# Attention and gated experts in one kernel: P summed in place, row maxima transposed on VectorE, 512-key tiles, 20 P buffers and a new order

## The chip, the cores and the metric

The kernel runs on one core of one Trainium2 chip. The metric is the device time of one execution in microseconds; a run's figure is that of its only core. "Before" is the median of three runs.

## What is computed

First an attention over 8 batches and 8 heads, with 1152 keys, head size 64, and queries averaged in pairs to 576. Its output, laid out as 8 x 576 x 512, goes into a layer of four causal attention experts, of which each token uses two, with weights from a gate.

```python
# attention
q_pool = q.reshape(B, H, S // 2, 2, D).mean(axis=3)          # 8, 8, 576, 64
scores = scale * np.matmul(q_pool, k.transpose(0, 1, 3, 2))  # ..., 576, 1152
scores = scores - np.max(scores, axis=-1, keepdims=True)
attn = np.exp(scores)
attn = attn / (np.sum(attn, axis=-1, keepdims=True) + 1e-09)
x = np.matmul(attn, v)        # then heads side by side: 8, 576, 512
# experts: 4 heads of 64, causal, top 2 of 4 by x @ w_gate
q, k, v = x @ wq[e], x @ wk[e], x @ wv[e]
a = softmax(where(causal, -1e9, scale * q @ k.T))
out += mask[..., None] * w[:, :, kk:kk + 1] * (a @ v @ wo[e])
```

## The kernel before

The kernel works on 32 *head pairs* p: two heads stand one above the other on the 128 partitions, 64 rows each. Every four head pairs make one batch b, whose expert part follows while later head pairs already run.

**Precision by splitting.** A 32-bit matrix product is made from rounded parts: K is `kh` plus the rest `kl`, Q is `qh` plus `ql`. Scores are kh·qh + kl·qh + kh·ql, and a fourth matmul (`ON` with `RM`) subtracts the row maximum. So each pair of matmuls (one for each head) appears four times for a chunk of 128 keys and a half of the queries (256 or 320, `QB`).

**One head pair, in stages.**

- `f_loadq`, `f_loadk`, `f_loadv` issue loads on SP's queue. K comes in three tiles of 384 keys. `f_prepq` adds the two queries of a pair on VectorE, ScalarE rounds the sum to `qh`, VectorE subtracts for `ql`; `f_prepk` makes `kh` on ScalarE and `kl` on GpSimd. `QD` holds the last 64 queries of both heads side by side.
- `f_max` computes rough scores kh·qh, 128 queries x 384 keys for each head, into PSUM (`gen`, eight banks), and VectorE reduces each to a column of maxima in `PM` (`row_max`, L602). `f_mxs` does the same for `QD` with one full-size matmul.
- `f_rows` takes the maximum over the three tiles (L648, `nm`), transposes it on TensorE with an identity matrix (L652), copies the rows to SBUF on VectorE (L657, `nt`), and two DMAs put them into rows 0 and 64 of `RM`.
- `f_st` makes the transposed scores of a half of the queries, one or two key chunks at a time, and ScalarE writes the exponentials into a P buffer (`pt`, L696). There are 11 P buffers (`NPT`).
- `f_av` multiplies P with V (L362, accumulated in one bank over nine chunks) and adds P to `sacc` (`add_up`): the first chunk is copied there by ScalarE (L371), the other eight are added by GpSimd (L379). A P buffer is free when both have read it.
- `g_norm`, after the ninth chunk: VectorE folds `sacc` by 32 columns and transposes (`fold32`, L739), a small matmul with `fold` sums over partitions (L764, the denominators), then a reciprocal, a transpose and a product; `f_xfin` splits the result into `x`.

**The experts** (`f_qk`, `f_vproj`, `f_mmax`, `f_mst`, `f_mask`, `f_mav`, `f_yfin`, `f_out`) take the same steps for each batch: projections in 12 matmuls each (L346), maxima with the causal mask (L1001), exponentials (L1044), a triangle cut on GpSimd (L1063), and the output product.

**What sets the order.** All these are Python generators ("flows"). A loop at the end of the kernel function picks, at each step, the flow that is ready first by an estimate of each engine's clock (`clk`, advanced by `emit` with a cost for each instruction), and writes its instructions down. A flow has a mode A, B or C by the shape of its matmuls: A for 64 rows x 128 columns (`rows2`, L355), B for 128 x 64 (`cols2` L362, and L764), C for 128 x 128 (`mm` L346, and L652). The loop prefers flows of the mode that it is in. `PLAN` has a row of 13 numbers for every half head pair (`GR` = 2) with thresholds for this choice: how long to wait for a flow of the present mode, how many P chunks must wait before a switch to P·V, when maxima and experts are due. A `Ring` is a set of buffers; a flow that needs one is not ready before the estimate says that one is free.

Of the kernel before, what the change touches and what calls it, by code (L numbers as in the profile page):

```python
# [17 lines left out]
SQ = 576  # L18
NKC = 9
# [12 lines left out]
NPT, NSA = 11, 3  # L32
# [29 lines left out]
    (0.2, 0.3, 0.6, 6, 4, 2.0, 0.12, 0.02, 3, 4.5, 3.9, 4.6, 4.55),  # L62
    (0.2, 0.3, 0.6, 6, 4, 2.0, 0.12, 0.02, 3, 4.5, 3.9, 4.6, 4.55),
    (0.15, 0.45, 0.2, 1, 2, 1.4, 0.25, 0.04, 2, 4.05, 3.9, 4.05, 4.1),
    (0.15, 0.45, 0.2, 1, 2, 1.4, 0.25, 0.04, 2, 4.05, 3.9, 4.05, 4.1),
    (0.2, 0.6, 0.6, 2, 4, 0.7, 0.25, -0.04, 1, 4.05, 3.9, 4.6, 4.1),
    (0.05, 0.3, 0.6, 4, 2, 0.9, 0.3, -0.04, 4, 4.05, 3.9, 4.6, 4.1),
    (0.05, 0.3, 0.6, 4, 2, 0.9, 0.3, -0.04, 4, 4.05, 3.9, 4.6, 4.1),
    (0.05, 0.3, 0.6, 4, 2, 0.9, 0.3, -0.04, 4, 4.05, 3.9, 4.6, 4.1),
    (0.2, 0.6, 0.6, 2, 4, 0.7, 0.25, -0.02, 1, 4.5, 3.9, 4.6, 4.1),  # L70
    (0.2, 0.6, 0.6, 2, 4, 0.7, 0.25, -0.02, 1, 4.5, 3.9, 4.6, 4.1),
    (0.05, 0.3, 0.6, 4, 2, 0.9, 0.3, -0.04, 4, 4.05, 3.9, 4.6, 4.1),
    (0.15, 0.45, 0.2, 1, 2, 1.4, 0.25, 0.04, 2, 4.05, 3.9, 4.05, 4.1),
    (0.05, 0.3, 0.6, 4, 2, 0.9, 0.3, -0.04, 4, 4.05, 3.9, 4.6, 4.1),
    (0.05, 0.3, 0.6, 4, 2, 0.9, 0.08, -0.04, 4, 4.05, 3.9, 4.6, 4.1),
    (0.1, 0.45, 0.3, 4, 2, 2.0, 0.12, 0.06, 1, 4.05, 3.9, 4.05, 4.1),
    (0.1, 0.45, 0.3, 4, 2, 2.0, 0.12, 0.06, 1, 4.05, 3.9, 4.05, 4.1),
    (0.05, 0.3, 0.6, 4, 2, 0.9, 0.3, -0.04, 4, 4.05, 3.9, 4.6, 4.1),
    (0.05, 0.3, 0.6, 6, 2, 0.9, 0.3, -0.04, 2, 4.05, 3.9, 4.6, 4.1),
    (0.05, 0.3, 0.6, 6, 2, 0.9, 0.3, -0.04, 2, 4.05, 3.9, 4.05, 4.1),  # L80
    (0.05, 0.3, 0.6, 4, 2, 0.9, 0.3, -0.04, 4, 4.05, 3.9, 4.6, 4.1),
    (0.05, 0.3, 0.6, 4, 2, 0.9, 0.3, -0.04, 4, 4.05, 3.9, 4.6, 4.1),
    (0.05, 0.3, 0.6, 4, 2, 0.9, 0.3, -0.04, 4, 4.05, 3.9, 4.6, 4.1),
    (0.05, 0.3, 0.6, 4, 2, 0.9, 0.3, -0.04, 4, 4.05, 3.9, 4.05, 4.1),
    (0.15, 0.45, 0.1, 2, 2, 1.2, 0.02, -0.3, 3, 4.05, 2.9, 4.6, 4.55),
    (0.1, 0.6, 0.45, 1, 2, 0.7, 0.3, -0.2, 3, 4.5, 2.9, 4.05, 4.75),
    (0.05, 0.3, 0.6, 6, 2, 0.9, 0.3, -0.04, 2, 4.05, 3.9, 4.05, 4.1),
    (0.05, 0.3, 0.6, 6, 2, 0.9, 0.3, -0.04, 2, 4.05, 3.9, 4.05, 4.1),
    (0.05, 0.3, 0.6, 4, 2, 0.9, 0.3, -0.04, 4, 4.05, 3.9, 4.05, 4.1),
    (0.05, 0.3, 0.6, 4, 2, 0.9, 0.3, -0.04, 4, 4.05, 3.9, 4.05, 4.1),  # L90
    (0.05, 0.3, 0.6, 4, 2, 0.9, 0.3, -0.04, 4, 4.05, 3.9, 4.05, 4.1),
    (0.1, 0.3, 0.2, 3, 2, 1.0, 0.12, -0.3, 2, 4.5, 2.9, 4.05, 4.75),
    (0.1, 0.3, 0.2, 3, 2, 1.0, 0.12, -0.3, 2, 4.5, 2.9, 4.05, 4.75),
    (0.05, 0.3, 0.6, 4, 2, 0.9, 0.3, -0.04, 4, 4.05, 3.9, 4.05, 4.1),
    (0.05, 0.1, 0.45, 3, 2, 1.2, 0.02, -0.3, 2, 4.05, 2.9, 4.6, 4.55),
    (0.05, 0.3, 0.6, 4, 2, 0.9, 0.3, -0.04, 4, 4.05, 3.9, 4.05, 4.1),
    (0.05, 0.3, 0.6, 4, 2, 0.9, 0.3, -0.04, 4, 4.05, 3.9, 4.05, 4.1),
    (0.05, 0.3, 0.6, 4, 2, 0.9, 0.3, -0.04, 4, 4.05, 3.9, 4.05, 4.1),
    (0.05, 0.3, 0.6, 4, 2, 0.9, 0.08, -0.04, 4, 4.05, 3.9, 4.6, 4.1),
    (0.05, 0.3, 0.6, 4, 2, 0.9, 0.08, -0.04, 4, 4.05, 3.9, 4.6, 4.1),  # L100
    (0.05, 0.3, 0.6, 6, 2, 0.9, 0.3, -0.04, 4, 4.05, 3.9, 4.05, 4.1),
    (0.15, 0.1, 0.2, 1, 1, 1.0, 0.02, -0.1, 4, 4.05, 3.9, 4.05, 4.55),
    (0.2, 0.6, 0.6, 1, 3, 1.2, 0.02, -0.3, 2, 4.5, 3.9, 4.6, 4.1),
    (0.05, 0.3, 0.6, 6, 1, 0.9, 0.3, -0.04, 4, 4.05, 3.9, 4.05, 4.1),
    (0.05, 0.3, 0.6, 6, 1, 0.9, 0.3, -0.04, 4, 4.05, 3.9, 4.05, 4.1),
    (0.05, 0.3, 0.6, 6, 2, 0.9, 0.3, -0.04, 4, 4.05, 3.9, 4.05, 4.1),
    (0.05, 0.3, 0.6, 6, 2, 0.9, 0.3, -0.04, 4, 4.05, 3.9, 4.05, 4.1),
    (0.05, 0.3, 0.6, 4, 2, 0.9, 0.08, -0.04, 4, 4.05, 3.9, 4.6, 4.1),
    (0.15, 0.3, 0.2, 2, 2, 2.0, 0.08, -0.2, 0, 4.5, 3.9, 4.05, 4.75),
    (0.05, 0.3, 0.6, 4, 2, 0.9, 0.08, -0.04, 4, 4.05, 3.9, 4.6, 4.1),  # L110
    (0.05, 0.3, 0.6, 4, 2, 0.9, 0.08, -0.04, 4, 4.05, 3.9, 4.6, 4.1),
    (0.2, 0.3, 0.6, 6, 4, 2.0, 0.12, 0.02, 3, 4.5, 3.9, 4.6, 4.55),
    (0.2, 0.3, 0.6, 6, 4, 2.0, 0.12, 0.02, 3, 4.5, 3.9, 4.6, 4.55),
    (0.05, 0.3, 0.6, 4, 2, 0.9, 0.08, -0.04, 4, 4.05, 3.9, 4.6, 4.1),
    (0.05, 0.3, 0.6, 6, 2, 0.9, 0.3, -0.04, 2, 4.05, 3.9, 4.05, 4.1),
    (0.05, 0.3, 0.6, 6, 2, 0.9, 0.3, -0.04, 2, 4.05, 3.9, 4.05, 4.1),
    (0.1, 0.45, 0.6, 6, 3, 1.0, 0.08, -0.1, 2, 4.05, 3.9, 4.6, 4.55),
    (0.05, 0.45, 0.6, 6, 2, 0.9, 0.3, -0.04, 2, 4.5, 3.9, 4.05, 4.1),
    (0.1, 0.45, 0.6, 2, 1, 1.0, 0.25, 0.06, 1, 4.05, 2.9, 4.6, 4.1),
    (0.05, 0.3, 0.6, 6, 2, 0.9, 0.3, -0.04, 2, 4.05, 3.9, 4.05, 4.1),  # L120
    (0.05, 0.1, 0.6, 1, 2, 1.0, 0.3, -0.2, 2, 4.5, 3.9, 4.6, 4.55),
    (0.05, 0.1, 0.6, 1, 2, 1.0, 0.3, -0.2, 0, 4.5, 3.9, 4.6, 4.75),
    (0.15, 0.3, 0.6, 3, 1, 0.7, 0.45, -0.3, 3, 4.05, 2.9, 4.6, 4.55),
    (0.1, 0.3, 0.45, 3, 3, 0.7, 0.02, -0.2, 0, 4.5, 3.9, 4.6, 4.1),
    (0.1, 0.3, 0.45, 3, 3, 0.7, 0.02, -0.2, 0, 4.5, 3.9, 4.6, 4.1),
    (0.15, 0.3, 0.6, 3, 1, 0.7, 0.45, -0.3, 3, 4.05, 2.9, 4.6, 4.55),
# [5 lines left out]
class Res:  # L132
# [6 lines left out]
    def __getitem__(self, i):  # L139
        return self.ap[i]  # L140

# [13 lines left out]
class Ring:  # L155
# [7 lines left out]
    def new(self):  # L163
        t = min(self.slots)
        self.slots.remove(t)
        self.live += 1
        self.n += 1

        r = Res(self.pool.tile(self.shape, self.dt, tag=f"{self.tag}{t[3]}", name=f"{self.tag}_{self.n}", bufs=1), self)
        _, r.u, r.ue, r.slot = t  # L170
        return r
# [17 lines left out]
def pooled_attention_then_moe_kernel(ctx: ExitStack, tc: tile.TileContext, qT, kT, vP, wall, wop, out):  # L189
# [64 lines left out]
    r_sacc = ring("sacc", [128, 640], F32, NSA)  # L254
    r_part = ring("part", [128, 20], F32, 4)
    r_kraw = ring("kraw", [128, 384], F32, 3)
# [3 lines left out]
    r_kh = ring("kh", [128, 384], F32R, 8)  # L260
    r_kl = ring("kl", [128, 384], F32R, 6)
    r_v = ring("v", [128, 3, 128], F32, 6)
    r_nm = ring("nm", [128, 2 * NQC], F32, 2)
    r_nt = ring("nt", [2 * NQC, 128], F32R, 2)
    r_accs = ring("accs", [128, 320], F32, 3)
    r_r9 = ring("r9", [128, 10], F32, 2)
# [102 lines left out]
    def act_first(o, i, n, R, W):  # L369

        nc.scalar.activation(o, i, AF.Copy, bias=1e-9 / 128, scale=1.0)  # L371
        emit("ACT", n / 1200 + 0.083, R, W)
# [880 lines left out]
```

## Time and profile before

| | |
|---|---|
| median of 3 runs (lowest to highest) | 1174.4 us (1174.08 to 1174.66) |
| the profiled execution | 1174.46 us, span 1172.7 us |
| granted TensorE clock | 0.997 |
| TensorE matmul / VectorE / ScalarE / GpSimd busy | 1137.2 / 883.6 / 700.6 / 969.5 us |
| DMA | 70.30 MB, mean 60 GB/s |

The page gives one execution. "PE" is TensorE's matmuls, "PEld" its weight loads, DVE is VectorE, ACT ScalarE, POOL GpSimd, SP the engine that issues the loads. A row of a group reads: line, engine, operation, output <- inputs with shapes, count, then busy time in us and mean ns of one, then idle time of the engine just before and what ended it. A row of the waits has who waited, for whom, then us in total, how often, and the longest. A row of the timeline has start and length in us and how many equal instructions were merged. A 32-bit matmul whose operands aren't rounded (P·V, denominators, transposes) leaves two records.

### The profile page before, as it was taken

To read this page: it belongs to the slowest core of one execution; us is meant where nothing else is said; L and a number is where in the kernel's file an instruction comes from. 1 tells how busy PE (TensorE), PEld (TensorE's weight loads), DVE (VectorE), ACT (ScalarE), POOL (GpSimd) and SP (SyncE) were. 2 spreads that over 40 slices of the span, in tenths; PEclk is the share of its full clock that TensorE was granted. 3 is DMA by queue.
4 is the path that set the end of the run, shared out by engine and by line. 5 is a ranking of instruction groups with operands and counts; after the bars stand their busy time and mean duration, and the time that the engine had idled before them with its cause. 6 is when DMAs were issued, how large, how long until landed. Compare 5 with 4: busy or idle time off the path is not lost.

```text
span 1172.7 us, 29459 instructions
## 1 busy us (share of the span) xinstructions
PE 1137.2 (97%) x11233; PEld 885.1 (75%) x11233; DVE 883.6 (75%) x2120; ACT 700.6 (60%) x2036; POOL 969.5 (83%) x839
## 2 busy tenths in 40 slices
PE   7999999999999999999999999999999999999997
PEld 5666787778877787777877788777887678777685
DVE  6998777786787867878588676978667876676675
ACT  4576645766466664676547755567645675556634
POOL 4899997988789977899689985899886997979922
PEclk9999999999999999999999999999999999999999
DMA  4223220121121211213102221112211123200011
GB/s 153 82 87 98 63 62 24 47 92 62 63 62 29 95 48 62 63 55 105 42 22 63 80 81 57 29 49 80 80 43 34 56 65 98 62 22 2 2 37 46
DMA packets 40569, 70.30 MB, mean 60 GB/s; under 512 B 4886, under 2 KB 31724, under 8 KB 40428
## 3 DMA queue, kind: packets, MB, share of 16 engines
q1 hardware_dynamic: 40284, 68.29, 18.7%
q8 instruction: 88, 1.44, 0.5%
q14 instruction: 53, 0.43, 0.1%
q10 hardware_dynamic: 144, 0.13, 0.0%
HBM read 58.73 MB, written 9.44 MB: 58 GB/s over the span
## 4 chain that ended last, share of the span: by engine, by line
PE 67%; POOL 20%; DVE 8%; issue 3%; ACT 2%; DMA 1%; POOLq 0%; SPq 0%; DVEq 0%; ACTq 0%
PE gen L355 30%; PE gen L362 19%; POOL sacc L379 18%; PE gen L346 17%; DVE PM L602 3%; POOL kl L379 1%; DVE gen L1001 1%; DVE part L739 1%; ACT pt L696 1%; PE gen L764 1%; POOL pt L1063 1%; PE gen L652 0%; DMA qraw<-in_qT 0%; DVE MPM L1001 0%; DVE qraw L375 0%
## 5 line engine op out<-in xcount | busy, mean ns | idle before, releaser
L379 POOL TENSOR_TENSOR sacc<-sacc,pt 128x512 f32<-128x512 f32 (+3 forms) x583 | 821.4, 1415 | 124.0 <-ACT sacc L371 81.9
L602 DVE TENSOR_REDUCE PM<-gen 128x1 f32<-128x384 f32 x864 | 425.6, 547 | 129.6 <-PE gen L355 108.5
L696 ACT ACTIVATE pt<-gen 128x320 f32<-128x320 f32 (+1 forms) x1152 | 383.1, 434 | 146.2 <-PE gen L355 140.6
L362 PE MATMUL gen<-pt,v 128*64 128x320 f32 (+4 forms) x2752 | 358.7, 404 | 1.2 <-POOL pt L1063 0.8
L362 PEld LDWEIGHTS gen<-pt,v 128*64 128x64 f32 (+1 forms) x2752 | 186.5, 137 | 118.2 <-issue 11.0
L355 PE MATMUL gen<-qh,kh 64*128 64x320 f32 (+1 forms) x1152 | 224.8, 322 | 2.9 <-DVE PM L602 1.7
L355 PE MATMUL gen<-qh,kl 64*128 64x320 f32 (+1 forms) x1152 | 207.8, 300 | 0.0
L355 PE MATMUL gen<-ql,kh 64*128 64x320 f32 (+1 forms) x1152 | 199.7, 293 | 0.0
L355 PE MATMUL gen<-RM,ON 64*128 64x320 f32 (+1 forms) x1152 | 199.7, 293 | 0.0
L355 PE MATMUL gen<-kh,qh 64*128 64x384 f32 x768 | 163.7, 378 | 8.7 <-ACT qh L366 7.0
L355 PEld LDWEIGHTS gen<-qh,kh 64*128 64x128 f32 x1152 | 143.0, 186 | 37.6 <-issue 12.4
L355 PEld LDWEIGHTS gen<-RM,ON 64*128 64x128 f32 x1152 | 138.9, 187 | 0.0
L355 PEld LDWEIGHTS gen<-ql,kh 64*128 64x128 f32 x1152 | 138.6, 187 | 0.0
L355 PEld LDWEIGHTS gen<-qh,kl 64*128 64x128 f32 x1152 | 134.3, 186 | 0.0
L355 PEld LDWEIGHTS gen<-kh,qh 64*128 64x128 f32 x768 | 91.6, 188 | 46.9 <-issue 23.5
L379 POOL TENSOR_TENSOR kl<-kraw,kh 128x384 fp32r<-128x384 f32 x96 | 102.0, 1082 | 7.2 <-ACT pt L696 4.1
L739 DVE TRANSPOSE_TENSOR_REDUCE part<-sacc 128x16 f32<-128x512 f32 (+1 forms) x96 | 73.5, 771 | 42.1 <-POOL sacc L379 41.7
L346 PE MATMUL gen<-x,WH 128*128 128x320 f32 (+1 forms) x512 | 103.6, 297 | 0.0
L346 PEld LDWEIGHTS gen<-x,WH 128*128 128x128 f32 x512 | 82.1, 188 | 0.8 <-issue 0.4
L1001 DVE CUSTOM_DVE_ANT_0 gen<-gen,mqk 64x288 f32<-64x288 f32 (+4 forms) x160 | 74.3, 502 | 7.9 <-PE gen L355 6.7
L346 PE MATMUL gen<-x,WL 128*128 128x320 f32 (+1 forms) x256 | 75.6, 295 | 0.0
L1044 ACT ACTIVATE pt<-gen 128x320 f32<-128x320 f32 (+2 forms) x224 | 64.0, 388 | 17.5 <-PE gen L355 16.9
(117 smaller groups left out, 1495.2 us busy)
## 6 DMA issues: line engine op xcount, KB each, us to landing
kraw<-in_kT SPq DMA_DIRECT2D x96, 192.0 KB
v<-in_vP SPq DMA_DIRECT2D x96, 192.0 KB
qraw<-in_qT SPq DMA_DIRECT2D x31, 576.0 KB
out<-ob SPq DMA_DIRECT2D x28, 256.0 KB
wst<-in_wall SPq DMA_DIRECT2D x8, 193.0 KB
RM<-nt SPq DMA_DIRECT2D x62, 2.5 KB
out<-ob SPq DMA_DIRECT2D x6, 128.0 KB
out<-pt SPq DMA_DIRECT2D x3, 256.0 KB
```

The lines of the kernel that those rows point to most:

```text
L346: nc.tensor.matmul(o, lhsT, rhs, start=start, stop=stop)
L355: nc.tensor.matmul(o(j), l(HEAD[j]), r(HEAD[j]), start=i == 0, stop=i == len(terms) - 1)
L362: nc.tensor.matmul(o(HEAD[j]), l(j), r(j), start=start, stop=stop)
L379: nc.gpsimd.tensor_tensor(o, a, b, op=op)
L602: nc.vector.tensor_reduce(pm[:, i, t:t + 1], ps[:, :384], axis=AX.X, op=ALU.max)
L696: nc.scalar.activation(pts[i][:, j, :qn], st[j][:, qn * i:qn * i + qn], AF.Exp, scale=0.0625)
L739: nc.vector.tensor_reduce(out, src.rearrange("p a (b r) -> p a b r", r=32), axis=AX.X, op=ALU.add, apply_transpose=True)
L764: nc.tensor.matmul(den[HEAD[j], 400:400 + k], fold, part[:, j * k:j * k + k], start=True, stop=True)
L1001: nc.vector.tensor_tensor_reduce(p, p, mqk[:m, 384 + m - w:384 + m], 1.0, LOW, ALU.add, ALU.max, pm[:m, j, c, i:i + 1])
L1044: nc.scalar.activation(pt_[:kn, j, f:qn], st[j][:kn, o - n:o], AF.Exp, scale=0.125)
L1063: nc.gpsimd.affine_select(out=sq, in_=sq, compare_op=ALU.is_ge, fill=0.0, base=0, pattern=[[0, 2], [1, kn]], channel_multiplier=-1)
```

## The change

1. **P summed in place.** `sacc` and its copy on ScalarE are gone. The P buffer of chunk 0 becomes the accumulator, kept until the fold; GpSimd adds the other chunks to it. The small constant that the copy had added to every entry is now added to the folded column by one tiny ScalarE instruction between the fold and the denominators' matmul (L809).
2. **Some chunks folded by VectorE.** `fold_in`: when the planner's clock for GpSimd is more than `OFP` = 3.0 us past that of TensorE (or of the chunk) and VectorE's is not, VectorE folds that chunk by itself into a further slot of `part` (up to three for a half), and the slots are added up before the denominators.
3. **Maxima transposed on VectorE.** `f_rows` reduces into two groups of columns of a 32-column `nm`, VectorE transposes it in blocks of 32 x 32, and four DMAs put the blocks in place. The transpose on TensorE and the copy from PSUM are gone.
4. **q split from PSUM.** VectorE sums the two queries into a PSUM bank, by halves, with a reduce over an axis of two; `qh`, `QD` and `ql` read that bank.
5. **K in tiles of 512, 512 and 128 keys** (the first head pair keeps 384). The maxima of four query chunks over the 128-key tile share a bank and one reduce.
6. **20 P buffers** for 11, 6 + 3 and 4 + 2 of `kh`/`kl` for 8 and 6; a smaller reserve for DMA descriptors.
7. **New order.** Another `PLAN`, some cost constants changed, and new orders of maxima within a head pair.

```diff
-NPT, NSA = 11, 3
+NPT, NKH = 20, 6
+NSL, OFP, OFD = 4, 3.0, 0.0
...
-    (0.2, 0.3, 0.6, 6, 4, 2.0, 0.12, 0.02, 3, 4.5, 3.9, 4.6, 4.55),
+    (0.2, 0.6, 0.1, 6, 1, 1.0, 0.25, -0.04, 0, 4.5, 2.9, 4.6, 4.1),
...
+    KT = lambda p: ((0, 384), (384, 384), (768, 384)) if p == 0 else ((0, 512), (512, 512), (1024, 128))
...
 def f_prepq(p, q):
-        any_tt(q[:, 0, :], q[:, 0, :], q[:, 1, :], ALU.add, SQ, [q], [q])
...
-        any_tt(ql.ap, q[:, 0, :], qh.ap.bitcast(F32), ALU.subtract, SQ, [q, qh], [ql])
+        for i, (a, n) in enumerate(QB):
+            qs, c = r_gen.new(), slice(a, a + n)
+            nc.vector.tensor_reduce(qs[:, :n], q[:, :, c].rearrange("p a q -> p q a"), axis=AX.X, op=ALU.add)
...
+            dve_tt(ql[:, c], qs[:, :n], qh[:, c].bitcast(F32), ALU.subtract, n, [qs, qh], [ql])
...
 def f_max(p):
+            seq = [((c,), t) for t in range(2) for c in range(NQF)] + [(range(NQF), 2)]
...
 def f_rows(pm, srcs, k, R, flags, col):
-        nc.tensor.transpose(ps[:n, :128], nm[:, :n], ident)
-        nc.vector.tensor_copy(nt[:n, :], ps[:n, :128])
+        for j, src in enumerate(srcs):
+            nc.vector.tensor_reduce(nm[:, k * j:k * j + k], src, axis=AX.X, op=ALU.max, negate=True)
+        nc.vector.transpose(nt.bitcast(F32), nm.bitcast(F32))
...
-        for r, k, part, col in dst:
-            mv(R[part:part + 1, col:col + 128 * k].rearrange("o (c q) -> o c q", c=k), nt[r:r + k, :], [nt], [R])
+        rows = R[:, col:col + 128 * k].rearrange("(h z) (c g q) -> z g h c q", h=2, c=k, g=4)
+        for g in range(4):
+            mv(rows[0, g], nt[32 * g:32 * g + 2 * k, :], [nt], [R])
...
 def f_av(p, c, hf, pt):
-            SACC[p, hf] = r_sacc.new()
+            SACC[p, hf] = pt
...
-        add_up(sacc, pt, 0, n, n, c, pool_tt)
-        pt.free()
+        if c and not fold_in(sacc, pt, n):
+            add_up(sacc, pt, 0, n, n, pool_tt)
+        if c:
+            pt.free()
...
+    def fold_in(sacc, pt, n):
+        if clk["POOL"] < max(clk["PE"], pt.rw) + OFP or clk["DVE"] > max(clk["PE"], pt.rw) + OFD:
+            return False
...
+        fold32(part[:, part.m, :2 * k].rearrange("p (a b) -> p a b", a=2), pt[:, :, :n], 2 * n, [pt], [part])
+        part.m += 1
+        return True
...
 def g_norm(acc, sacc, n, box, gate=None):
+        nc.scalar.activation(part[:, m, :2 * k], part[:, m, :2 * k], AF.Copy, bias=1e-9 / 128, scale=1.0)
```

How the order changes is seen in the programs themselves. The first place is TensorE's queue. Before, in the expert part of a middle batch, two maximum matmuls (A), a transpose (C), eight P·V matmuls (B) and again maxima and scores (A) follow each other; `mqh`, `mkh`, `MRM` are the experts' q, k and row maxima, `gen` the PSUM banks.

```order
L355 MATMUL gen_5703<-kh_4983,qh_5019 128x384
L355 MATMUL gen_5704<-kh_4983,qh_5019 128x384
L652 MATMUL gen_5709<-ident,nm_5559 10x128
L362 MATMUL gen_5713<-pt_5645,v_5096 64x256 x2
L362 MATMUL gen_5713<-pt_5646,v_5096 64x256 x2
L362 MATMUL gen_5722<-pt_5675,v_2_4615 64x320 x2
L362 MATMUL gen_5722<-pt_5690,v_2_4615 64x320 x2
L355 MATMUL gen_5732<-kh_4983,qh_5019 128x384
L355 MATMUL gen_5733<-kh_4983,qh_5019 128x384
L355 MATMUL gen_5740<-qh_4594,kh_4436 128x256
```

Here is TensorE in the changed program, in the same batch: behind a long run of scores come the three `QD` matmuls (C) and then the denominators and a whole half of P·V (B).

```order
L375 MATMUL gen_5616<-RM_95,ON 128x256
L375 MATMUL gen_5617<-RM_95,ON 128x256
L366 MATMUL gen_5632<-kh_24_4683,QD_102 128x512
L366 MATMUL gen_5635<-kh_25_4754,QD_102 128x512
L366 MATMUL gen_5638<-kh_11_4984,QD_102 128x128
L814 MATMUL gen_5641<-part_5495,fold 64x8 x2
L382 MATMUL gen_5650<-pt_5459,v_4809 64x256 x2
L382 MATMUL gen_5650<-pt_5460,v_4809 64x256 x2
L382 MATMUL gen_5650<-pt_5497,v_4809 64x256 x2
L382 MATMUL gen_5650<-pt_5498,v_4811 64x256 x2
L382 MATMUL gen_5650<-pt_5528,v_4811 64x256 x2
L382 MATMUL gen_5650<-pt_5529,v_4811 64x256 x2
```

The transpose is out of TensorE's queue, and P·V stands together. Over the whole program the mode changes 357 times before and 172 times after; the longest A runs are 102 matmuls before, and many of 168 to 184 after.

The second place is VectorE's queue around a head pair's maxima. Before, the maxima of the next head pair (`PM_99`) and a fold stand between the reduce into `nm` and the copy `nt` of the transposed rows.

```order
L602 TENSOR_REDUCE PM_100<-gen_4819 128x1
L648 TENSOR_REDUCE nm_4824<-PM_100 128x9
L602 TENSOR_REDUCE PM_99<-gen_4852 128x1
L602 TENSOR_REDUCE PM_99<-gen_4853 128x1
L602 TENSOR_REDUCE PM_99<-gen_4871 128x1
L602 TENSOR_REDUCE PM_99<-gen_4872 128x1
L602 TENSOR_REDUCE PM_99<-gen_4890 128x1
L602 TENSOR_REDUCE PM_99<-gen_4891 128x1
L739 TENSOR_REDUCE part_4896<-sacc_4712 128x16
L657 CAST nt_4900<-gen_4898 9x128
```

After, on the same engine, the two reduces and the transpose follow the last of the maxima at once.

```order
L556 TENSOR_REDUCE gen_4651<-qraw_4299 128x320
L390 TENSOR_TENSOR mkl_4634<-gen_4635,mkh_4633 128x256
L630 TENSOR_REDUCE PM_100<-gen_4658 128x1
L390 TENSOR_TENSOR ql_4628<-gen_4651,qh_4627 128x320
L630 TENSOR_REDUCE PM_100<-gen_4662 128x1
L630 TENSOR_REDUCE PM_100<-gen_4665 128x1
L677 TENSOR_REDUCE nm_121<-PM_100 128x5 x2
L681 STREAM_TRANSPOSE nt_4670<-nm_121 128x32
```

The way from the maxima to `nt` no longer leaves VectorE. Counted over the programs, GpSimd's sums of 640 elements a partition go from 285 to 212, those of 512 from 256 to 251; folds on VectorE go from 96 to 171, maxima from 864 to 678 instructions, and SP's DMAs of maxima from 98 to 196.

## Prediction before the run

> **What bounds the kernel now.** I read the page first: busy time by engine, then the chain of waits.
>
> ```profile
> span 1172.7 us, 29459 instructions
> PE 1137.2 (97%) x11233; PEld 885.1 (75%) x11233; DVE 883.6 (75%) x2120; ACT 700.6 (60%) x2036; POOL 969.5 (83%) x839
> PE 67%; POOL 20%; DVE 8%; issue 3%; ACT 2%; DMA 1%; POOLq 0%; SPq 0%; DVEq 0%; ACTq 0%
> ```
>
> TensorE is busy for 97% of the span and carries two thirds of the chain; GpSimd comes next. The 97% counts a matmul until its modelled end, so time lost between matmuls hides inside it. Starts of matmuls show it, so the second view is the timeline of PE. The program uses the array in three shapes: 64 rows x 128 columns (L355: scores and row maxima; I call it A), 128 x 64 (L362 and L764: P times V, and the denominators; B), and 128 x 128 (L346 and L652: projections, QD, transposes; C).
>
> ```profile
> 364.85 0.47 PE L355 MATMUL gen<-kh,qh 64*128 64x384 f32 x2
> 365.25 0.87 PE L362 MATMUL gen<-pt,v 128*64 128x256 f32 x8
> 366.05 0.44 PE L355 MATMUL gen<-kh,qh 64*128 64x384 f32 x2
> 366.33 0.31 PE L355 MATMUL gen<-qh,kh 64*128 64x320 f32 x2
> ...
> 368.09 0.25 PE L355 MATMUL gen<-mqh,mkh 64*128 64x192 f32 x2
> 368.18 0.28 PE L355 MATMUL gen<-mqh,mkl 64*128 64x192 f32 x2
> 368.29 0.27 PE L355 MATMUL gen<-mql,mkh 64*128 64x192 f32 x2
> ...
> 368.52 0.35 PE L355 MATMUL gen<-kh,qh 64*128 64x384 f32 x2
> 368.71 0.22 PE L355 MATMUL gen<-mqh,mkh 64*64 64x128 f32 x2
> ...
> 369.29 0.31 PE L355 MATMUL gen<-ql,kh 64*128 64x320 f32 x2
> 369.44 0.31 PE L355 MATMUL gen<-RM,ON 64*128 64x320 f32 x2
> 369.68 0.28 PE L652 MATMUL gen<-ident,nm 128*9 128x128 f32 x1
> 369.71 0.42 PE L346 MATMUL gen<-kh,QD 128*128 128x384 f32 x1
> 370.07 0.76 PE L362 MATMUL gen<-pt,v 128*64 128x320 f32 x4
> ```
>
> Read the first column. Inside a run of one shape a 384-column pair is followed after 0.19 us (368.52 to 368.71) and a 320-column pair after 0.15 (369.29 to 369.44). Where the shape changes it takes longer: A to B 0.40 instead of 0.19 (364.85 to 365.25), B to A 0.28 instead of 0.19 (seen on the first pair behind it, 366.05 to 366.33), A to C 0.24 instead of 0.15, C to B 0.36 where the 384-column pace is 0.19. The extra is 0.21, 0.09, 0.09 and 0.17: 0.14 us a change on average. In the program's order on PE the shape changes 357 times. So about 50 us of a "busy" PE is this.
>
> The third view is the waits, for what PE itself waits on.
>
> ```profile
> DVE part L739 <- POOL sacc L379: 41.7, 38, 4.2
> PEld gen L355 <- DVE PM L602: 18.2, 63, 1.1
> PE gen L764 <- DVE part L739: 9.7, 15, 1.4
> PEld gen L764 <- DVE part L739: 6.7, 12, 1.5
> ```
>
> The denominators (L764) wait for VectorE's fold, and the fold waits for the last of GpSimd's sums. The maxima (L602) hold PSUM that the next matmul wants. Nothing else holds PE for more than single microseconds, apart from the first 7 us of loading and the end.
>
> **The change, part by part.** The profiled execution took 1174.46 us, its span 1172.7; the median of the runs shown is 1174.4, so the sum is made from 1174.5.
>
> *New order and 20 P buffers.* A run of A needs one P buffer for each key chunk, so 11 buffers end it after at most 11 chunks; with 20 a whole head pair (18 chunks) goes through. Counted in the two orders, the changes of shape fall from 357 to 172: 185 fewer at 0.14 us is 26 us. Bounds: every change at the cheapest, 0.09, gives 17; at the dearest, 0.21, gives 39. I take 26. This is on PE's own line, so nothing hides it.
>
> *Transposes of the row maxima.* The 49 L652 matmuls go. The one above lets the next start after 0.03 us; its whole record is 0.28. So between 1 and 14 us; the start is the better measure of what a queued engine loses, and the waits around it are counted as changes of shape: 3 us. In their place come one more small reduce (49, see L648 below) and a VectorE transpose, beside the old CAST's place, and four DMAs for two. Those are on the path maxima, row in RM, next head pair's scores, and stand on SP's in-order queue ahead of later K, V and Q loads.
>
> ```profile
> L648 DVE TENSOR_REDUCE nm<-PM 128x9 f32<-128x27 f32 x31 | 5.7, 183 | 1.1
> L396 SPq DMA_DIRECT2D RM<-nt x62: 652/700/896, 48.0 to 1071.5; - x62
> L779 DVE STREAM_TRANSPOSE gen<-r 128x256 f32<-128x256 f32 x48 | 22.1, 460 | 3.5
> ```
>
> Two more issues are 1.4 us a set; 98 more in all are 69 us of SP's time. After the new order's last maxima (QD) stands a run of about 40 B matmuls, 8 us at the pace of the eight records at 365.25 (0.80 us; a B matmul leaves two records). The path is three maxima (L602 below, 0.55 each), two small reduces, a transpose of at most 0.46, four issues: 1.65 + 0.36 + 0.46 + 2.8 = 5.3 us, plus a landing that these rows don't show. Hidden, with some 2 us over: 0. If that cover is gone it is a rival below. For the loads behind them on SP:
>
> ```profile
> SPq L396 <- DVE nt L657: 160.5, 13, 25.8
> ACT kh L366 <- DMA kraw<-in_kT: 19.3, 18, 3.4
> ```
>
> SP already stands 160 us behind a late `nt`, K loads with it, and ScalarE waited 19 us in all for K, PE for no load. Another 1.4 us in front of a load is lost in that: 0.
>
> *K in 512-key tiles.* For a query chunk the maxima go from three 384-column pairs to two of 512 and one of 128. At 0.15 us per 320 columns a 512 pair is 0.24. For a pair of 128 there is no row; by columns it is 0.06, but 192-column pairs already stand at 0.09 to 0.11, so up to 0.11; I take that, the nearest row. 3 x 0.19 = 0.57 becomes 0.59, or at worst 0.54 becomes 0.59: 0 to +6 us over 31 x 4 chunks, QD's 31 sets up to 2 more. I take +5. The Trainium skill (TensorE: Matmul & The Clock Gate, Back-to-back issue gap) gives a sustained 81 ns for a matmul of 128 columns and 131 for 512. By its figures old and new come out level (an estimate, interpolating 384), and the sum would be 5 us lower; but its figure for a pair of 384 would be about 0.23 where the row has 0.19, so the rows stand.
>
> *P summed in place, folds on VectorE, q.* These are off PE. Their price by group:
>
> ```profile
> L379 POOL TENSOR_TENSOR sacc<-sacc,pt 128x640 f32<-128x640 f32 x285 | 461.8, 1623 | 38.8 <-ACT sacc L371 22.7 <-DVE gate L916 1.0
> L379 POOL TENSOR_TENSOR sacc<-sacc,pt 128x512 f32<-128x512 f32 x256 | 330.4, 1291 | 76.8 <-ACT sacc L371 57.4 <-ACT pt L696 3.6 <-DVE PM L602 0.7
> L602 DVE TENSOR_REDUCE PM<-gen 128x1 f32<-128x384 f32 x864 | 425.6, 547 | 129.6 <-PE gen L355 108.5 <-PE gen L346 16.2
> L739 DVE TRANSPOSE_TENSOR_REDUCE part<-sacc 128x20 f32<-128x640 f32 x48 | 40.3, 841 | 24.4 <-POOL sacc L379 24.1
> L371 ACT ACTIVATE sacc<-pt 128x640 f32<-128x640 f32 x48 | 36.8, 767 | 0.1
> L375 DVE TENSOR_TENSOR qraw<-qraw 128x576 f32<-128x576 f32 x31 | 38.8, 1252 | 10.8 <-DMA qraw<-in_qT 10.8
> L375 DVE TENSOR_TENSOR ql<-qraw,qh 128x576 fp32r<-128x576 f32 x31 | 35.5, 1145 | 4.5 <-ACT qh L366 4.5
> L375 DVE TENSOR_TENSOR x<-gen,x 128x320 fp32r<-128x320 f32 x32 | 15.4, 481 | 4.7 <-ACT x L366 4.5
> ```
>
> GpSimd: the order holds 212 sums of 640 for 285 and 251 of 512 for 256: 73 x 1.62 + 5 x 1.29 = 125 us less of 969. ScalarE: 96 copies go (0.77 for the wide ones), 96 tiny ones come. VectorE: 75 more folds (171 for 96) at up to 0.84 = 62 us; 35 small reduces and 49 more nm ones at 0.18 = 15; 678 maxima for 864 on the same columns, so only the fixed part of 186 goes, somewhere between 0 and 0.2 us each, say 20; q goes from 1.25 + 1.15 to a sum over 1152 values, by L602's 547 for 384 about 1.64, and 0.9 for the remainder from PSUM (by L375 x): +4. Net about +60, to 945 us. None of this is PE's time. What reaches PE is the wait for the last sum: with 125 us off GpSimd I take 10 of the 16.4 us that L764 waited for `part`. Ends: all 16 gone, or 10 more, where each of the 96 den pairs waits 0.1 us for the ScalarE step that now stands between the fold and it, in order behind exponentials. And with 21 instead of 27 maximum tiles a pair the 18.2 us behind `PM` shrink by a quarter: 4 (ends 9 and 0).
>
> Sum: 1174.5 - 26 - 3 + 5 - 10 - 4 = 1136.5. **Forecast 1136 us.** With each term at its better or worse half this case spans 1118 to 1152.
>
> **The rivals.**
>
> *The long runs starve on VectorE.* In A runs two engines must keep pace with PE, and VectorE gets more to do. Three such runs of today, by window:
>
> ```profile
> 627.30:632.90 5.60, 5.60 (x88) 5.42 (x86) 3.75 (x8) 4.53 (x16) 5.37 (x5) 1.00 0.15 41
> 677.40:684.70 7.30, 7.30 (x82) 6.62 (x80) 7.18 (x18) 6.61 (x18) 6.91 (x7) 1.00 0.01 2
> 752.60:761.00 8.40, 7.73 (x88) 6.78 (x88) 8.28 (x18) 6.62 (x19) 5.97 (x10) 1.00 0.11 27
> ```
>
> The columns are PE, PEld, VectorE, ScalarE, GpSimd, with counts. With VectorE at 3.75 of 5.60 us the matmuls come every 64 ns, with it full (7.18 of 7.30, 8.28 of 8.40) every 89 and 95. Some 3 ns of that are the wider matmuls; the rest, about 25 ns, is waiting. The change has 6,464 A matmuls, as before. If 17% more of them than today run at VectorE's pace, that is 6,464 x 0.17 x 0.025 = 28 us: **1164**. For it: +60 us on VectorE, and runs that give it no pause. Against: fewer, wider maxima, and a B run of 8 us behind each long A run in which VectorE catches up. The Trainium skill (SBUF — State Buffer, Door 1: The DMA port swizzle) says that an access that crosses to a new 16-byte line pays; the new q sum steps 2304 bytes between its two terms, which would bear on this case. No row of before shows such a read. Were the sum to take twice its 1.64 us, VectorE would have 51 us more.
>
> *More goes than I count.* Changes at 0.21, no added cost of the 512 tiles, the waits for `part` and half of those for `PM` gone: 1174.5 - 39 - 3 - 16 - 9 = **1107**. For it: 0.14 rests on four places, and with GpSimd lighter the fold may never be late.
>
> *The row path comes late (slower).* Place: the first scores of each of 31 head pairs, which read RM. If VectorE is over 2 us behind when QD's maxima are queued, the B run no longer covers the path; then the two extra issues, 1.4 us, and 0.4 us of extra VectorE steps are in the open each time: 31 x 1.8 = 56, giving **1192**. It decides where the lag passes those 2 us; no wait of PE for RM shows in before, against it.
>
> That the change doesn't do what it says can be put aside: the order shows the folds, the missing transposes and the 172 changes of shape.
>
> **How the numbers follow.** Forecast 0.59, starving runs 0.18, more gained 0.15, late rows 0.08. About 0.2% is what a measurement of this kernel can tell from no change. Starving runs spread from 1150 to 1182, so a quarter of that case is not faster: faster 0.87, same 0.03, slower 0.10. The range 1104 to 1172 takes in the first three cases but for that tail.
>
> **What would show it.** Right: starts at a change of shape still 0.1 to 0.2 us apart from the pace, GpSimd near 845, VectorE near 945, ScalarE near 655, waits of L764's successor for `part` under 10 us. Wrong: VectorE at 97% or more in most long A windows with matmuls 85 ns apart (starving); PE idle ahead of the first scores of a head pair behind a DMA into RM or a late `nt` (late rows); or a PE that reaches the pace of 64 ns in the long runs, with nothing left of the waits (more gained).

## The result and the profile after

The changed kernel takes **1123.1 us** (median of 4 runs, 1122.1 to 1123.6) against 1174.5 us of the kernel before on the same chip: a ratio of 0.956, 95% interval 0.9545 to 0.9578. The gain is 51.5 us where 38 were forecast; the time lies in the range, and inside the narrower one of the forecast's own case (1118 to 1152).

The page of the changed kernel, with the span, the busy times and the chain of waits:

```profile
span 1121.9 us, 29476 instructions
PE 1096.4 (98%) x11184; PEld 879.1 (78%) x11184; DVE 919.7 (82%) x2160; ACT 654.7 (58%) x2067; POOL 826.1 (74%) x761
PE 74%; DVE 20%; issue 2%; POOL 1%; ACT 1%; DMA 1%; DVEq 0%; POOLq 0%; ACTq 0%
PE gen L375 31%; PE gen L382 22%; PE gen L366 20%; DVE PM L630 8%; DVE part L767 3%; DVE gen L1051 2%; POOL pt L394 1%; PE gen L814 1%; DVE gen L556 1%; DVE gen L829 1%; DMA kraw<-in_kT 1%; DVE gen L390 1%; DVE WL L390 1%; DVE x L390 0%; DVE MPM L1055 0%
```

GpSimd has gone from 20% of the chain to 1%, and VectorE from 8% to 20%. TensorE's "busy" share hardly moved although the span is 51 us shorter: with only 49 matmuls fewer its busy time fell by 41 us, so most of the lost time was inside the busy time, as the prediction took it. The busy times were forecast at 845 (GpSimd), 945 (VectorE) and 655 (ScalarE) and are 826, 920 and 655.

The groups behind those sums, line by line (busy time, mean ns of one, idle before):

```profile
L394 POOL TENSOR_TENSOR pt<-pt,pt 128x640 f32<-128x640 f32 x212 | 332.6, 1569 | 28.1 <-ACT pt L1094 13.7 <-DVE pt L390 0.8 <-PE gen L814 0.7
L394 POOL TENSOR_TENSOR pt<-pt,pt 128x512 f32<-128x512 f32 x251 | 323.4, 1289 | 35.7 <-PE gen L382 13.2 <-PE gen L814 5.2
L630 DVE TENSOR_REDUCE PM<-gen 128x1 f32<-128x512 f32 x558 | 345.7, 679 | 53.2 <-PE gen L375 43.4 <-PE gen L366 9.4
L767 DVE TRANSPOSE_TENSOR_REDUCE part<-pt 128x20 f32<-128x640 f32 x118 | 95.7, 826 | 10.1 <-POOL pt L394 10.1
L556 DVE TENSOR_REDUCE gen<-qraw 128x320 f32<-128x640 f32 x31 | 25.8, 833 | 0.0
L556 DVE TENSOR_REDUCE gen<-qraw 128x256 f32<-128x512 f32 x31 | 21.7, 699 | 0.7 <-ACT pt L722 0.7
```

The waits that the prediction named, in the changed kernel (in all, times, longest):

```profile
DVE part L767 <- POOL pt L394: 15.4, 11, 4.8
PEld gen L375 <- DVE PM L630: 14.7, 49, 0.9
PEld gen L814 <- ACT part L809: 7.7, 15, 1.6
PE gen L814 <- ACT part L809: 2.5, 3, 1.2
```

The fold waited 41.7 us for GpSimd before and waits 15.4 now; the rows of the denominators' waits for `part` add up to 16.4 us before and 10.2 now. (A matmul and its weight load often wait through the same time; counted once, it is 14.5 and 7.7.)

**Where the 51 us came from, by starts.** I took every distance from one matmul's start to the next one's in both traces and subtracted the pace that a matmul of its shape and width keeps in an undisturbed run (0.147 us for a pair of 320 columns, 0.110 for a pair of 128). What is left over falls from 159.5 us to 103.4: at changes of shape from 67.5 to 36.0, inside runs of A from 55.5 to 48.3, inside runs of B from 22.5 to 12.3, inside runs of C from 14.1 to 6.8. So some 31 us stand at changes of shape, 25 are shorter waits elsewhere, and about 5 were given back in undisturbed pace. The figure at a change contains any wait that happens to end there; the experiments price the change alone.

### The profile page after: what moved, and what is told of

Same layout as the page of the kernel before. It is cut to its first block, busy times and chain, and to the rows that moved or that the text cites. A ratio compares the mean times of both kernels' runs of the same rounds, so it can differ in the third digit from the quotient of the medians.

```text
span 1121.9 us, 29476 instructions
## 1 busy us (share of the span) xinstructions
PE 1096.4 (98%) x11184; PEld 879.1 (78%) x11184; DVE 919.7 (82%) x2160; ACT 654.7 (58%) x2067; POOL 826.1 (74%) x761
## 4 chain that ended last, share of the span: by engine, by line
PE 74%; DVE 20%; issue 2%; POOL 1%; ACT 1%; DMA 1%; DVEq 0%; POOLq 0%; ACTq 0%
PE gen L375 31%; PE gen L382 22%; PE gen L366 20%; DVE PM L630 8%; DVE part L767 3%; DVE gen L1051 2%; POOL pt L394 1%; PE gen L814 1%; DVE gen L556 1%; DVE gen L829 1%; DMA kraw<-in_kT 1%; DVE gen L390 1%; DVE WL L390 1%; DVE x L390 0%; DVE MPM L1055 0%
## 5 line engine op out<-in xcount | busy, mean ns | idle before, releaser
L394 POOL TENSOR_TENSOR pt<-pt,pt 128x512 f32<-128x512 f32 (+4 forms) x503 | 682.9, 1363 | 69.9 <-PE gen L382 15.7
L630 DVE TENSOR_REDUCE PM<-gen 128x1 f32<-128x512 f32 (+3 forms) x678 | 403.1, 656 | 91.4 <-PE gen L375 46.1
L382 PE MATMUL gen<-pt,v 128*64 128x320 f32 (+3 forms) x2752 | 343.6, 402 | 0.5 <-DVE MPM L1051 0.2
L375 PE MATMUL gen<-qh,kl 64*128 64x320 f32 (+1 forms) x1152 | 222.8, 302 | 0.0
L375 PE MATMUL gen<-ql,kh 64*128 64x320 f32 (+1 forms) x1152 | 213.4, 294 | 0.0
L375 PE MATMUL gen<-kh,qh 64*128 64x512 f32 (+2 forms) x768 | 147.9, 367 | 7.6 <-ACT qh L386 7.0
L375 PEld LDWEIGHTS gen<-qh,kl 64*128 64x128 f32 x1152 | 148.1, 187 | 3.1
L767 DVE TRANSPOSE_TENSOR_REDUCE part<-pt 128x20 f32<-128x640 f32 (+1 forms) x171 | 131.6, 785 | 15.4 <-POOL pt L394 15.4
L394 POOL TENSOR_TENSOR kl<-kraw,kh 128x512 fp32r<-128x512 f32 (+2 forms) x96 | 95.9, 1015 | 61.8 <-PE gen L375 22.1
L386 ACT COPY accs<-gen 128x256 f32<-128x256 f32 (+1 forms) x96 | 38.5, 401 | 66.5 <-PE gen L382 65.8
```

The source lines that it names most:

```text
L375: nc.tensor.matmul(o(j), l(HEAD[j]), r(HEAD[j]), start=i == 0, stop=i == len(terms) - 1)
L382: nc.tensor.matmul(o(HEAD[j]), l(j), r(j), start=start, stop=stop)
L386: nc.scalar.copy(o, i)
L394: nc.gpsimd.tensor_tensor(o, a, b, op=op)
L630: nc.vector.tensor_reduce(pm[:, i:i + k, t], ps[:, :n * k].rearrange("p (c n) -> p c n", c=k), axis=AX.X, op=ALU.max)
L767: nc.vector.tensor_reduce(out, src.rearrange("p a (b r) -> p a b r", r=32), axis=AX.X, op=ALU.add, apply_transpose=True)
```

## The experiments

The theory at the outset (T): about 31 of the 51.5 us come from 185 fewer changes of shape. Its rival (F): a change of shape costs nothing by itself, and a lighter GpSimd is the gain. All 12 runs, in order of time, with before and the change for comparison; each was timed against the kernel before on its chip:

| run | changes of shape | us | ratio to before (95%) | granted clock |
|---|---|---|---|---|
| before | 357 | 1174.5 | | 0.997 |
| the change | 172 | 1123.1 | 0.956 (0.9545-0.9578) | 0.997 |
| e_shapesame | 172 | 1127.6 | 0.959 (0.9580-0.9609) | 0.997 |
| e_shape64r | 360 | 1153.0 | 0.982 (0.9803-0.9836) | 1.000 |
| e_tinyA | 172 | 1162.4 | 0.990 (0.9884-0.9917) | 0.998 |
| e_after_oldplan | 245 | 1162.8 | 0.990 (0.9882-0.9912) | 0.994 |
| e_after_pt19 | 209 | 1172.6 | 0.999 (0.9979-0.9998) | 0.979 |
| e_oldplan_pt14 | 308 | 1202.1 | 1.024 (1.0227-1.0258) | 0.983 |
| e_after_nofold | 223 | 1217.3 | 1.036 (1.0345-1.0376) | 0.966 |
| e_after_pt14 | 248 | 1219.1 | 1.038 (1.0360-1.0405) | 0.972 |
| e_after_tensort | 245 | 1240.3 | 1.054 (1.0507-1.0572) | 0.966 |
| e_before_newplan | 317 | 1240.7 | 1.056 (1.0529-1.0585) | 0.974 |
| e_tinyC | 725 | 1250.8 | 1.065 (1.0636-1.0668) | 0.992 |
| e_foldpool | 172 | 1260.8 | 1.074 (1.0718-1.0754) | 0.954 |

### What a change of shape costs, among P·V

```diff
 # in g_norm, behind the two matmuls of the denominators
+        nc.tensor.matmul(den[:, 420:430], ident[:64, :], ident[:64, :10], start=True, stop=True)    # e_shape64r
+        nc.tensor.matmul(den[:64, 420:430], fold, ident[:, :10], start=True, stop=True)             # e_shapesame
```

> The changed kernel with one more tiny matmul (64 rows, 10 columns, into a part of the denominators' bank that nobody reads) behind each of the 96 accumulations of the denominators; it adds nothing to the result. The run of matmuls there is of the shape of P times V (128 rows, 64 columns), so each tiny matmul adds two changes of shape: 360 in place of 172. Nothing else moves on any engine. Theory T (about 31 of the 51.5 us come from having 185 fewer changes of shape, at 0.14 to 0.21 us each): 188 x 0.14 to 0.21 = 26 to 39 us above the control run with the tiny matmul in the neighbours' shape, so 1153 to 1168 us. Rival F (a change of shape by itself costs nothing; the gain came from shorter waits behind a lighter GpSimd): within 3 us of the control, about 1128 us.

> The control: the same 96 tiny matmuls (10 columns), but in the shape of their neighbours (128 rows, 64 columns), so that the number of changes of shape stays 172. It adds nothing to the result. Both theories: 96 matmuls of 0.03 to 0.07 us each, 3 to 7 us, so 1126 to 1130 us.

1153.0 (1148.7 to 1155.1) against 1127.6 (1125.6 to 1128.2): 25.4 us for 188 more changes, **0.135 us each**, at the low end of what T gave. F's figure, within 3 us of the control, falls: nothing but the tiny matmul differs between the two. Its shape has a price of its own beside the change, though, and the control doesn't hold that: its weight loads take 184 ns for the control's 139, and the 64-row control of the next section cost 0.136 us each where this one's cost 0.047 (4.5 us for 96). If all of 0.136 is taken off, the 29.9 us above the change leave 0.09 us a change. One place in the timeline of the run with 64-row matmuls (start, length, then what; each 32-bit matmul leaves two records):

```profile
507.58 0.24 PE L814 MATMUL gen<-part,fold 128*64 128x10 f32 x4
507.75 0.39 PE L816 MATMUL gen<-ident 64*128 64x10 f32 x2
508.07 1.52 PE L382 MATMUL gen<-pt,v 128*64 128x256 f32 x12
```

and such a place in the control:

```profile
518.22 0.29 PE L814 MATMUL gen<-part,fold 128*64 128x10 f32 x4
518.36 0.20 PE L816 MATMUL gen<-ident,fold 128*64 128x10 f32 x1
518.36 0.48 PE L382 MATMUL gen<-pt,v 128*64 128x320 f32 x1
518.41 0.20 PE L816 MATMUL gen<-ident,fold 128*64 128x10 f32 x1
518.47 0.73 PE L382 MATMUL gen<-pt,v 128*64 128x320 f32 x3
```

From the tiny matmul's first record to the first P·V that has it whole behind it: 508.07 - 507.75 = 0.32 us against 518.47 - 518.36 = 0.11; and 0.17 against 0.14 ahead of it. The two changes together are worth 0.2 to 0.3 us in the place itself.

### The same among the scores

```diff
     def rows2(o, terms, R, W, tiny=None):
...
+            if tiny is not None and i == len(terms) - 1:
+                nc.tensor.matmul(tiny[:, 400:410], ident, ident[:, :10], start=True, stop=True)                # e_tinyC
+                nc.tensor.matmul(tiny[:, 400:410], ident[:64, :], ident[:64, :10], start=True, stop=True)      # e_tinyA
```

> The changed kernel with one more tiny matmul of the projections' shape (128 rows, 128 columns, 10 columns moved) behind the scores of each of the 288 chunks of 320 queries, into a part of their bank that nobody reads; it adds nothing to the result. It splits the runs of scores: 725 changes of shape in place of 172; nothing else moves on any engine. If a change costs here what it cost among the matmuls of P times V: 553 x 0.135 = 75 us above its control (by the bounds of the forecast, 0.09 to 0.21: 50 to 116 us). Rival: in runs of scores ScalarE and VectorE set the pace, so that most of it is hidden: under 40 us.

> The control of the run with 288 tiny matmuls among the scores: the same number in the scores' own shape (64 rows), so that the changes stay 172. It adds nothing to the result. 288 matmuls of 0.03 to 0.06 us each: +9 to +17 us, 1132 to 1140 us; less where scores wait anyway.

1250.8 against 1162.4: 88.4 us for 553 changes, **0.160 us each**; up to 7.5 us of it may be the granted clock, 0.992 for 0.998 (an estimate), which leaves 0.147. The rival falls: ScalarE and VectorE don't hide a change in a run of scores. The weight loads of the tiny matmuls show where some of the time goes (first the run with 128 rows, then its control; busy time, mean ns, idle before):

```profile
L377 PEld LDWEIGHTS gen<-ident 128*128 128x128 f32 x576 | 86.9, 190 | 55.8 <-issue 55.8
L377 PEld LDWEIGHTS gen<-ident 64*128 64x128 f32 x576 | 96.5, 186 | 0.0
```

The loads take the same time, but at a change of shape they begin late: 55.8 us idle for 288 tiny matmuls is 0.19 us each, where the control has none. The control itself was missed: 39 us for its 288 matmuls, 0.136 each, where 0.03 to 0.06 were expected. A lone 64-row matmul between pairs is dear here: by the starts, the first record comes 0.139 us (median) behind the last of the scores, whose own pace is 0.073. So a tiny matmul isn't small change everywhere, and without a control the price would have read 0.23.

### Fewer P buffers, and no early folds

```diff
-NPT, NKH = 20, 6
+NPT, NKH = 14, 6                # e_after_pt14
-NSL, OFP, OFD = 4, 3.0, 0.0
+NSL, OFP, OFD = 4, 1e9, 0.0     # e_after_nofold
```

> The changed kernel with 14 P buffers in place of 20 and nothing else edited; the planner then cuts the matmuls into shorter runs: 248 changes of shape in place of 172, longest run of scores 130 matmuls in place of 184, and VectorE folds 212 chunks in place of 171, so that GpSimd is lighter still. Theory T: 76 x 0.14 to 0.21 = +11 to +16, 1134 to 1139 us. Rival F (the lighter GpSimd is the gain, whatever the number of changes): GpSimd's 32 fewer additions cannot hurt, 1120 to 1126 us.

> The changed kernel with no chunk folded early by VectorE: GpSimd makes all 587 additions, as it made 583 before the change, and VectorE folds only the 96 sums; the planner's order has 223 changes of shape in place of 172. Theory T: 51 x 0.14 to 0.21 = +7 to +11, and up to +5 for longer waits for the folded sums: 1130 to 1139 us. Rival F (the lighter GpSimd is the gain): most of the 51.5 us comes back, 1155 us or more.

Both theories fail on the first: it is slower than the kernel before by 44 us, though it has 109 changes fewer and a GpSimd that is busy 783.8 us. On the second T fails, and F's "1155 us or more" holds, but the loss is far more than the whole gain. In the run without early folds, TensorE's waits for the denominators are several times those of the changed kernel (7.7 and 2.5 us there):

```profile
DVE part L767 <- POOL pt L394: 68.5, 36, 12.7
PEld gen L814 <- ACT part L809: 37.2, 32, 6.1
PE gen L814 <- ACT part L809: 24.7, 17, 5.6
```

And the clock falls behind such waits. Three stretches of 20 us of that run (columns: PE, PEld, VectorE, ScalarE, GpSimd with counts, then the granted clock):

```profile
60.00:80.00 20.00, 18.85 (x198) 14.10 (x200) 13.25 (x25) 14.74 (x47) 19.06 (x15) 1.00 0.27 83
80.00:100.00 20.00, 13.32 (x105) 7.58 (x103) 18.40 (x29) 6.45 (x20) 19.14 (x14) 0.93 0.21 58
100.00:120.00 20.00, 13.22 (x136) 11.77 (x136) 13.23 (x26) 7.85 (x28) 12.02 (x9) 0.65 0.28 90
```

and the last two in the changed kernel:

```profile
80.00:100.00 20.00, 19.49 (x201) 13.64 (x199) 19.62 (x38) 12.95 (x41) 19.21 (x15) 1.00 0.44 131
100.00:120.00 20.00, 19.91 (x228) 15.39 (x226) 19.14 (x38) 12.72 (x42) 19.14 (x14) 1.00 0.19 60
```

GpSimd is at its limit in 80 to 100 in both (19.14 and 19.21 of 20). Where VectorE doesn't take chunks over, TensorE loses a third of its time and then its clock. If all of TensorE's time stretched with the clock, 0.966 over 1216.6 us would be 41 us, against 3 at 0.997; 51 changes at 0.135 are 7; of the 94 us above the changed kernel some 49 are left to the waits themselves. (An estimate: what the clock's fall costs was not measured by itself.) But both runs also have an order made anew, so the folds need a run in which the order stays.

### The folds given back to GpSimd, in the same order

```diff
 def fold_in(sacc, pt, n):
-        fold32(part[:, part.m, :2 * k].rearrange("p (a b) -> p a b", a=2), pt[:, :, :n], 2 * n, [pt], [part])
+        o = sacc[:, :, :n]
+        nc.gpsimd.tensor_tensor(o, o, pt[:, :, :n], op=ALU.add)
+        emit("DVE", 2 * n * 0.00112 + 0.054, [pt], [part])
 def g_norm(acc, sacc, n, box, gate=None):
-            m = NSL
-            nc.vector.tensor_reduce(part[:, m, :2 * k], part[:, :part.m, :2 * k].rearrange("p m k -> p k m"), ...)
```

> The changed kernel with its order of instructions kept as it is on every engine, except that each of the 75 chunks that VectorE folded early is added by GpSimd into the running sum at the same place in the program: GpSimd makes 75 additions more (75 x 1.36 = +102 us, to about 928), VectorE 75 folds less (75 x 0.78 = -58 us, to about 861). 172 changes of shape as before. It tells why the run without early folds came out at 1217 us, 94 us above the change, though its order was made anew. Theory P (GpSimd's lag itself: the denominators wait for sums that GpSimd finishes late, and TensorE waits with them): most of the 94 us is here too, 1160 to 1220 us. Theory O (the order that was made anew is what lost it): 1121 to 1133 us.

1260.8 us, 138 above the change and more than theory P gave; O falls here. The page and the waits of that run:

```profile
PE 1135.3 (91%) x11184; PEld 909.1 (73%) x11184; DVE 864.0 (69%) x2050; ACT 657.1 (52%) x2067; POOL 941.0 (75%) x836
PEclk9989899989999999899998899988999899999999
```

The second line, the granted clock in 40 slices, falls below 9 all over the run.

```profile
PEld gen L375 <- ACT pt L722: 99.8, 68, 6.5
ACT pt L722 <- POOL pt L785: 96.7, 33, 6.4
DVE part L767 <- POOL pt L785: 61.7, 12, 7.3
DVE part L767 <- POOL pt L394: 55.0, 21, 9.9
```

GpSimd is busy for only 75% of the span, and still holds everything: ScalarE waits 96.7 us for P buffers that GpSimd hasn't read, and the scores wait 99.8 us for ScalarE to empty their PSUM. These waits read as a full queue: the 20 P buffers stand between ScalarE and GpSimd, and the long runs of scores fill them. The 75 chunks that VectorE takes are few, and `fold_in` takes them where the planner has GpSimd more than 3 us behind. The 138 us are not all waiting: at a granted clock of 0.954, up to 55 us of them may be the clock (an estimate as above). So F is right in that the relief is indispensable, and wrong in that it is the gain: it is the condition under which the order with 172 changes can run. What remains open is what the best order without folds would give.

### The table of numbers by itself

The next two runs exchange the whole `PLAN` and nothing else: the changed kernel with the old table (shown by its first row), and the kernel before with the new one, the same edit turned round.

```diff
 PLAN = [
-    (0.2, 0.6, 0.1, 6, 1, 1.0, 0.25, -0.04, 0, 4.5, 2.9, 4.6, 4.1),
+    (0.2, 0.3, 0.6, 6, 4, 2.0, 0.12, 0.02, 3, 4.5, 3.9, 4.6, 4.55),
...
```

> The changed kernel in all its parts, with the table of numbers of the kernel before for the planner: 245 changes of shape in place of 172, 182 folds in place of 171, longest run of scores 178. By the number of changes alone, at the 0.135 us that the tiny matmuls gave: 73 x 0.135 = +10, 1133 us. Theory O (an order that does not fit the parts makes TensorE wait, and the clock falls behind the waits, as in the run with 14 P buffers): 1180 to 1225 us.

> The kernel before in all its parts (11 P buffers, 583 or so additions by GpSimd, transposes on TensorE) with the table of numbers of the changed kernel: 317 changes of shape in place of 357, longest run 108 matmuls in place of 102. By the number of changes alone: 40 x 0.135 = -5, 1169 us. Theory O: the order does not fit the parts, 1190 to 1260 us. If the table by itself were the gain: 1125 to 1140 us.

The changed parts with the old table: 1162.8 us, 1.0% better than before, between what the count of changes gave (1133) and theory O (1180 or more). The old parts with the new table: 1240.7 us, 66 *worse* than before, as theory O had it. So neither half is the gain: parts without the table give 12 of the 51.5 us, the table without the parts loses 66, together they give 51.5. The waits of the old parts with the new table show where some of it goes:

```profile
POOL sacc L379 <- ACT sacc L371: 103.7, 21, 11.5
DVE part L739 <- POOL sacc L379: 52.6, 45, 8.8
PEld gen L764 <- DVE part L739: 21.5, 24, 4.9
```

The chunks' way through the sums is the same as before, copy, additions, fold, denominators, and later at each step: GpSimd waits 103.7 us for ScalarE's copies (22.7 + 57.4 = 80.1 before), the fold 52.6 for GpSimd (41.7), the denominators 21.5 (6.7).

### Transposes on TensorE, one buffer fewer, and 14 buffers with the old table

```diff
-NPT, NKH = 20, 6
+NPT, NKH = 19, 6                # e_after_tensort, e_after_pt19
+NPT, NKH = 14, 6                # e_oldplan_pt14, with the old table
 def f_rows(...):                 # e_after_tensort
-        nc.vector.transpose(nt.bitcast(F32), nm.bitcast(F32))
+        nc.tensor.transpose(ps[:n, :128], nm[:, :n], ident)
+        nc.vector.tensor_copy(nt[:n, :], ps[:n, :128])
```

`e_after_tensort` puts `f_rows` of the kernel before back, and for lack of space takes a P buffer away; `e_after_pt19` only takes the buffer (`NPT` = 19); `e_oldplan_pt14` has the old table and `NPT` = 14.

> The changed kernel with the row maxima transposed on TensorE again (49 transposes more) and 19 P buffers in place of 20, since the space is short; 245 changes of shape in place of 172, 220 folds. By numbers alone: 73 x 0.135 = 10, and 49 transposes at 0.06 = 3, so 1136 us. Theory O (the order made anew for parts that the table was not chosen for): 1180 to 1225 us.

> The changed kernel with 19 P buffers in place of 20 and the table of numbers as it is: 209 changes of shape in place of 172, 176 folds in place of 171. By the number of changes alone: 37 x 0.135 = +5, 1128 us. Theory O (any order made for other parts than the table was chosen for loses far more than its changes): 1160 to 1240 us, and then the run with transposes on TensorE and 19 buffers tells nothing of the transposes.

> The changed kernel with the table of numbers of the kernel before and 14 P buffers in place of 20: 308 changes of shape, against 245 with the same table and 20 buffers (1162.8 us). By the number of changes alone: 63 x 0.135 = +8.5, 1171 us. If the buffers are worth more than the changes that they save (as GpSimd's slack): 1180 us or more.

One buffer out of 20 costs 49 us at this table (1172.6), far from the 5 of its changes. So the 1240.3 us of the run with transposes hold at least a misfit of that size, and say nothing sure about the transposes: that term stays unmeasured. With the old table, six buffers fewer cost 39 us (1202.1 against 1162.8), of which 63 changes at 0.135 are 8.5 and 0.983 for 0.994 of clock up to 13 (an estimate); the rest, some 18, is put down to waiting. Here too the buffers are worth more than the changes that they save.

## Why the prediction was right, and where its sizes were off

**Changes of shape, -26.** Right. The two prices, 0.135 and 0.160 us, stand beside the 0.14 that was read from four places; 185 of them are 25 to 30 us, and 17 at the 0.09 that is left if the tiny matmul's own time is taken off as above. The 31 us by the starts contain waits that end at a change.

**Waits for `part`, -10.** Right in sign, too small. The two rows that the prediction added up went from 16.4 to 10.2 us, 6 less, and 7 less (14.5 to 7.7) where a time that both rows hold is counted once. But the denominators had more rows, under other names, that the prediction left aside; these were in the kernel before:

```profile
PEld gen L764 <- issue: 7.4, 10, 1.9
PEld gen L764 <- ACT pt L696: 6.5, 15, 0.9
PEld gen L764 <- DVE PM L602: 3.3, 7, 1.6
```

and this is the largest of those left after:

```profile
PEld gen L814 <- issue: 1.1, 4, 0.4
```

With them, the rows of PE and PEld at the denominators add up to 40 us before and 12.5 after; each time counted once, 28.7 and 10.4. By the starts, a denominator behind P·V was 0.32 us late in 58 places (18.4 us) and is 0.19 late in 25 (4.8). So this term is -14 to -18 and not -10: it was mis-sized, and is 4 to 8 of the 13 us by which the forecast was too high. A wait's name says who came last; the place has to be summed over all names, and PE and PEld not added.

**`PM` waits, -4.** 18.2 to 14.7 us: right.

**Tiles of 512 and 128 keys, +5.** The pace of a 128-column pair, which had no row, is now in the timeline of the changed kernel: 0.40 us for seven matmuls, 0.114 a pair, against 0.11 taken.

```profile
600.19 0.45 PE L375 MATMUL gen<-RM,ON 64*128 64x320 f32 x2
600.33 0.58 PE L375 MATMUL gen<-kh,qh 64*128 64x128 f32 x7
600.73 0.36 PE L375 MATMUL gen<-qh,kh 64*128 64x320 f32 x1
```

The 5 us of worse pace found by the starts are this term, as far as it can be told. **Transposes, -3:** not settled, as said above.

With these sizes the sum is -17 to -30, -14 to -18, -4, +5 and -3: -33 to -50. The measured -51.5 lies a little beyond it. By the starts, runs of C lost 7 us less than before (14.1 to 6.8), for which the sum had no term; what was waited for there stays open.

**What the sum did not see.** It priced the lighter GpSimd at 10 us, as a wait that shrinks. In the new order it is a condition: without it the kernel takes 138 us more. The sum came out because the change has all its parts; as a statement of what each part is worth it would have been wrong, since 1162.8 and 1240.7 us show that the parts don't add.

**The rivals.** *Starving on VectorE* did not come. Stretches of the changed kernel with a long run of scores and with the run of P·V behind it (PE, PEld, VectorE, ScalarE, GpSimd, then the clock):

```profile
587.00:603.00 16.00, 15.94 (x194) 13.34 (x190) 15.53 (x27) 12.78 (x42) 15.37 (x11) 1.00 0.22 75
605.10:613.60 8.50, 8.50 (x74) 5.78 (x74) 8.20 (x26) 3.19 (x9) 8.03 (x7) 1.00 0.17 46
```

VectorE is full in both, 15.53 of 16 and 8.20 of 8.50, and matmuls come 82 ns apart in the first, not far from the sign of starving. Over the whole trace the sign is rare: of the 41 runs of 80 and more A matmuls behind the first 23 us, 12 have VectorE at 97% or more, and only 4 come 85 ns or more apart. Taken together these runs lose 7 to 8 ns a matmul over their pace, where 13 such runs lost 12 to 14 before. That VectorE catches up under P·V, as the counter-argument had it, fits the two rows but wasn't shown. *Late rows*: no wait of TensorE for a DMA into `RM` shows in the changed kernel; in the two runs with 14 buffers there are three, of 5.4 us in all. *More gained*, at 1107, was the nearest rival, and the time lies about half way to it. The rule on 16-byte lines (the Trainium skill, SBUF — State Buffer, Door 1: The DMA port swizzle), for which the prediction weighed a q sum of twice the time, does not show in this access: 640 values read 2304 bytes apart in pairs take 833 ns, 1.30 ns each, and a maximum over 512 contiguous ones from PSUM 679 ns, 1.33 each. The sum took 1.53 us a head pair for the forecast 1.64.

## What to carry to other kernels

On an engine that reads 98% busy, look at the distance between starts: a change of matmul shape was about 0.14 us here, and a pair of runs with a tiny matmul in two shapes prices it, as well as the control's own time is known. When an order is lengthened into runs, ask which queue the runs fill and who drains it: an engine busy for only 75% cost this kernel 138 us. And don't undo one part of a planned order to learn what the part is worth; the order then fits nothing, and one buffer in 20 reads as 49 us: keep the order and exchange the single instruction.

## What the runs showed of the hardware

The granted clock of TensorE goes with its waits. Leaving out the loading at the start, TensorE stood idle for over 1 us 10 to 34 times in the runs with a clock of 0.954 to 0.983, and 2 to 6 times in those with 0.992 to 1.000. In the run without early folds it looks like this: a stretch with a long wait, the two behind it (columns as above, the clock third from the end), and the matmul that waited.

```profile
90.00:97.00 7.00, 2.63 (x15) 1.29 (x13) 6.30 (x11) 3.13 (x9) 6.69 (x6) 1.00 0.13 40
100.00:114.00 14.00, 7.22 (x49) 5.83 (x51) 11.45 (x23) 1.85 (x7) 12.02 (x9) 0.50 0.26 76
114.00:120.00 6.00, 6.00 (x91) 5.94 (x89) 1.78 (x3) 6.00 (x22) 0.00 (x0) 0.99 0.34 121
97.47 0.39 PE L814 MATMUL gen<-part,fold 128*64 128x8 f32 x4 [4.83 <-ACT part L809]
```

The Trainium skill (TensorE: Matmul & The Clock Gate, Part 1: The HAM clock gate) has the array at half rate after an idle window of about 3.4 us. The 0.50 behind a wait of 4.83 us agrees. But the clock also fell where no single wait was that long: the longest of TensorE's matmuls, behind the start, is 2.7 us in the run with transposes on TensorE (3.0 of a weight load), and its clock is 0.966.

The start needs care. The row of the first 20 us of the same run (here PE, clock, DMA) reads 1.00, though TensorE waits 7.1 us there for the first `qh`. But the trace holds no clock record before 22.0 us, and time without a record counts as 1.00. The starts tell the clock there:

```profile
0.00:20.00 20.00, 10.57 (x55) 1.00 0.65 203
21.16 0.62 PE L375 MATMUL gen<-qh,kl 64*128 64x256 f32 x2
21.37 0.63 PE L375 MATMUL gen<-ql,kh 64*128 64x256 f32 x2
...
22.01 0.40 PE L375 MATMUL gen<-qh,kl 64*128 64x256 f32 x2
22.13 0.39 PE L375 MATMUL gen<-ql,kh 64*128 64x256 f32 x2
```

A pair of 256 columns is followed after 0.21 us before 22 us, and after 0.12 from there on: the first matmuls ran at about half rate.
